# Warm-up in single-pass products, no filler products, the sine table loaded later, and small products in full shape

## The chip, the cores and the metric

The kernel runs on one core of a Trainium2 chip. Its time is the device time of one execution in microseconds (us). The core has a matrix engine (TensorE, PE in the rows; its weight loads are listed apart as PEld), three engines for elementwise work (VectorE or DVE, ScalarE or ACT, GpSimd or POOL) and SP, which mostly starts transfers (DMA). TensorE runs at one of two granted clocks, 1.2 or 2.4 GHz. Three runs of the kernel before took 457.12 us in the median, from 455.9 to 459.17.

## The reference

Three stages follow each other on inputs of batch 2, sequence 768 and width 512 (8 heads of 64), all in fp32.

```
# 1 attention with decay, block by block of the sequence
intra = (q k^T * lam**(i-j) for j <= i) v;  inter = (q * lam**(i+1)) state
state = lam**block * state + (k * lam**(block-1-i))^T v
# 2 transform and feed-forward
u  = x + real(fft over sequence and width of x)
un = (u - mean(u)) / sqrt(var(u) + 1e-6)
x  = u + relu(un @ w_ch1) @ w_ch2            # 512 -> 2048 -> 512
# 3 gated value
gate = sigmoid(conv over 5 steps of x);  out = (gate * (x @ w_val)) @ w_out
```

## The kernel before, in words

The work goes through in three overlapping parts. **Attention** takes each batch in six chunks of 128 positions. A chunk is loaded by four transfers (`load_chunk`, L), and then has score products (`att_S`, S), a multiplication by the decay mask on DVE (`att_pm`, s; tile `pa`), products with v (`att_AV`, A), products with the state (`att_inter`, E) and an update of the state (`att_ST`, T). Chunks are loaded into a ring of three, so a load waits until an earlier chunk has been read. **The transform** of a batch is made of products with cosine and sine tables: `cd` over the width (`fft_D`, XD), `cos` and `sin` over the sequence (`fft_P`, `fft_Q`, XP, XQ), and two small parts, `fft_a384` (XA; what one middle position gives) and `fft_P256` (XK; one middle frequency). **Feed-forward** goes over four blocks of 384 positions (k = 0 to 3) and 16 slices of the 2048 hidden units: `ffn1` (F), relu with the rest to fp32 on DVE (f, h), `ffn2` (G). Before each block stands the norm: mean (Nm), centring (Nc), squares, `ln_var` (Nv, the variance by products with a column of ones) and the square root on DVE and ACT (Nw). Weights are loaded raw and converted on ACT and DVE (names with D). The second batch's attention and transform lie among the first batch's feed-forward.

Products are of two kinds. In fp32r a product is one record in the trace. In fp32 it is two records, and slower. The large products of blocks 1 to 3 are three fp32r products each (`mm3`); those of the transform, the attention and `ffn1` of block 0 are fp32.

The order of all instructions is written out by hand in ORDER, one token for each step: the letters name the method, the numbers its arguments. Each engine takes its instructions in this order, and waits for its operands. A buffer's next writer also waits for its last reader.

Four places matter here. In `setup` eight fp32 products of the identity with `ones` run while the first chunk is loaded, and their result is not read (the warm-up); `pe_fill` (token Z4) makes four more after the first scores. The sine table (`Xcs1`) is the first token of the order, so its transfer stands behind chunk 0. `fft_a384` and `ln_var` take products whose moving operand is a single column. `fft_fx`, `fft_fxh` and `fft_fxl` (Xx, Xh, Xl) make a row of sums and split it into two fp32r parts, which `fft_D` adds to its even half (w = 0) with two products of one row.

Of the kernel before, what the change touches and what calls it, by code (L numbers as in the profile page):

```python
# [34 lines left out]
WARM = 8  # L35
# [8 lines left out]
    "L": "load_chunk", "Z": "pe_fill", "K": "lam_powers", "S": "att_S", "s": "att_pm", "k": "att_kd_act", "A": "att_AV", "E": "att_inter", "T": "att_ST", "t": "att_st", "X": "x_shift",  # L44
    "Xcd": "fft_cd", "Xcs": "fft_cs", "XD": "fft_D", "XA": "fft_a384", "XQ": "fft_Q", "XP": "fft_P", "Xc": "fft_pc",
# [8 lines left out]
    "Kq": "att_qs", "Y": "att_decay", "Xm": "fft_pm", "Xe": "fft_edge", "Xo": "fft_fold", "Xx": "fft_fx", "Xl": "fft_fxl", "Xp": "fft_mp", "Xu": "u_add",  # L54
# [5 lines left out]
Xcs1 S0,0,0 S0,0,1 Z4 L0,1 s0,0,0 s0,0,1 K A0,0 k0,0,0 k0,0,1 L0,2 T0,0 Kq0,1+ e0,0+ k0,1,0 S0,1,0 S0,1,1 t0,0 k0,1,1 T0,1 Y0,1 s0,1,0 L0,3 s0,1,1 A0,1 a0,0 Kq0,2+ t0,1 k0,2,0 S0,2,0  # L60
# [51 lines left out]
class Kern:  # L112
# [16 lines left out]
    def setup(self):  # L129
# [43 lines left out]
        for x in range(2):  # L173
            nc.scalar.copy(self.oddr[:, x * C:(x + 1) * C], self.odd)
# [748 lines left out]
```

## Time and profile before

| | |
|---|---|
| median of three runs | 457.12 us |
| the profiled execution | 459.33 us |
| its span, first to last instruction | 457.5 us |
| mean granted clock of TensorE | 0.989 |
| PE busy | 447.6 us (98%) |
| DVE, ACT, POOL busy | 312.7, 244.6, 129.1 us |
| moved by DMA | 40.45 MB |

Durations come from the profiled execution. In a timeline row the first number is the start, the second the time from the first start to the last end of the merged instructions, and the bracket at the end, where there is one, the idle time before them and what ended it. The ends of products are modelled: a product is shown until its result has left the array, while the next has begun. What a stretch of products costs is therefore read from start to start.

### The profile page before, as it was taken

The numbers are of one execution on the slowest core, as the hardware profiler recorded it, in microseconds if no ns is written. First come the engines' busy times: TensorE is split into PE (matmuls) and PEld (weight loads), VectorE is DVE, ScalarE is ACT, GpSimd is POOL, SyncE is SP. The second block draws the span as 40 slices with busy tenths as digits, with TensorE's granted clock in tenths as the row PEclk, the third lists the DMA queues.
The fourth block names the chain that finished last, engine by engine and source line by source line (L and its number), as shares of the span: only waits on it lengthen the run. The fifth ranks groups of instructions, "written<-read, shape, count | busy, mean of one in ns | idle before, by whom it ended". The sixth has DMA issues, their size and how long they took to land.

```text
span 457.5 us, 7094 instructions
## 1 busy us (share of the span) xinstructions
PE 447.6 (98%) x2752; PEld 396.8 (87%) x2752; DVE 312.7 (68%) x498; ACT 244.6 (53%) x501; POOL 129.1 (28%) x115
## 2 busy tenths in 40 slices
PE   8999999999999999899999999999999999999996
PEld 7887757777658779899999999999999999999994
DVE  5768489887989998885866478813736794222594
ACT  4555566756757765486436357524733844242442
POOL 1132304201041112325263446322523512430230
PEclk9999899889999999999999999999999999999999
DMA  7899951547735340000000000000000010000101
GB/s 266 287 302 318 397 160 65 177 172 255 239 140 185 100 178 1 0 3 0 1 0 24 0 1 23 1 1 24 1 1 0 24 46 1 0 1 24 47 1 69
DMA packets 15861, 40.45 MB, mean 88 GB/s; under 512 B 2012, under 2 KB 4052, under 8 KB 14804
## 3 DMA queue, kind: packets, MB, share of 16 engines
q1 hardware_dynamic: 15540, 39.62, 25.0%
q8 instruction: 21, 0.34, 0.3%
q10 hardware_dynamic: 288, 0.39, 0.3%
q14 instruction: 12, 0.10, 0.1%
HBM read 35.29 MB, written 3.15 MB: 84 GB/s over the span
## 4 chain that ended last, share of the span: by engine, by line
PE 90%; DVE 4%; DMA 2%; SPq 1%; issue 1%; ACT 1%; DVEq 0%; ACTq 0%
PE acc L636 10%; PE acc L638 10%; PE acc L637 10%; PE ph L644 8%; PE ph L638 7%; PE ph L636 7%; PE ph L637 7%; PE pso L636 4%; PE pso L637 4%; PE pso L638 4%; PE pso L373 3%; PE psS L251 3%; PE pso L266 2%; PE pso L277 2%; PE pso L399 2%; PE pso L389 2%
## 5 line engine op out<-in xcount | busy, mean ns | idle before, releaser
L636 PE MATMUL acc<-g,w2s 128*128 128x384 f32 x240 | 83.5, 348 | 1.3 <-DVE tmp L680 1.3
L637 PE MATMUL acc<-g,w2s 128*128 128x384 f32 x240 | 80.5, 335 | 0.0
L638 PE MATMUL acc<-g,w2s 128*128 128x384 f32 x240 | 80.5, 335 | 0.0
L632 POOL TENSOR_TENSOR w2s<-w,w2s 128x512 fp32r<-128x512 f32 x27 | 36.9, 1366 | 145.2 <-ACT w2s L628 130.7
L628 ACT CAST w2s<-w 128x512 fp32r<-128x512 f32 x62 | 37.9, 618 | 42.7 <-PE acc L638 42.7
L665 DVE SCALAR_TENSOR_TENSOR g<-ph,g 128x384 fp32r<-128x384 f32 x60 | 32.8, 553 | 35.3 <-ACT g L660 34.8
L731 DVE SCALAR_TENSOR_TENSOR gate<-u,cw,gate 128x384 f32<-128x384 f32 (+4 forms) x64 | 48.4, 770 | 1.6 <-ACT gate L726 0.9
L636 PEld LDWEIGHTS acc<-g,w2s 128*128 128x128 f32 x240 | 45.1, 188 | 3.7 <-DVE tmp L680 1.6
L614 ACT CAST w1s<-w 128x512 fp32r<-128x512 f32 x48 | 29.6, 618 | 34.5 <-PE ph L638 34.3
L637 PEld LDWEIGHTS acc<-g,w2s 128*128 128x128 f32 x240 | 45.1, 188 | 1.3
L660 ACT ACTIVATE g<-ph 128x384 fp32r<-128x384 f32 x60 | 28.9, 488 | 30.6 <-PE acc L638 17.2
L638 PEld LDWEIGHTS acc<-g,w2s 128*128 128x128 f32 x240 | 45.1, 188 | 0.1
L644 PE MATMUL ph<-uc,w 128*128 128x384 f32 x128 | 45.1, 501 | 0.0
L636 PE MATMUL ph<-hlA,w1s 128*128 128x384 f32 x128 | 43.4, 339 | 0.6 <-DVE g L665 0.6
L638 PE MATMUL ph<-hlA,w1s 128*128 128x384 f32 x128 | 43.1, 337 | 0.2 <-DVE w1s L618 0.2
L637 PE MATMUL ph<-hlA,w1s 128*128 128x384 f32 x128 | 42.9, 335 | 0.0
L618 POOL TENSOR_TENSOR w1s<-w,w1s 128x512 fp32r<-128x512 f32 x21 | 28.2, 1347 | 50.7 <-ACT w1s L614 36.1
L632 DVE TENSOR_TENSOR w2s<-w,w2s 128x512 fp32r<-128x512 f32 x35 | 27.3, 779 | 21.9 <-ACT w2s L628 21.7
L644 PEld LDWEIGHTS ph<-uc,w 128*128 128x128 f32 x128 | 24.8, 197 | 15.0 <-issue 1.4
L618 DVE TENSOR_TENSOR w1s<-w,w1s 128x512 fp32r<-128x512 f32 x27 | 23.0, 859 | 18.6 <-ACT w1s L614 18.6
L636 PEld LDWEIGHTS ph<-hlA,w1s 128*128 128x128 f32 x128 | 24.0, 188 | 1.3 <-DVE g L665 0.9
L638 PEld LDWEIGHTS ph<-hlA,w1s 128*128 128x128 f32 x128 | 24.0, 188 | 0.8 <-DVE w1s L618 0.8
(212 smaller groups left out, 957.4 us busy)
## 6 DMA issues: line engine op xcount, KB each, us to landing
raw<-in_w_dram SPq DMA_DIRECT2D x16, 1024.0 KB, 5.0
ldqk<-in_qT_dram SPq DMA_DIRECT2D x12, 256.0 KB, 5.7
ldqk<-in_k_dram SPq DMA_DIRECT2D x12, 256.0 KB, 5.8
ldv<-in_v_dram SPq DMA_DIRECT2D x12, 256.0 KB, 5.8
ldkT<-in_kT_dram SPq DMA_DIRECT2D x11, 256.0 KB, 6.3
out_dram<-o SPq DMA_DIRECT2D x11, 256.0 KB, 2.0
raw<-in_wv_dram SPq DMA_DIRECT2D x2, 1024.0 KB, 5.0
raw<-in_wo_dram SPq DMA_DIRECT2D x2, 1024.0 KB, 4.7
```

Source lines behind the costliest of these rows:

```text
L251: nc.tensor.matmul(r["pss"][t][:, a, :], r["kT"][hp, a, :], r["qT"][hp, a, :], start=True, stop=True)
L614: self.nc.scalar.copy(w[:, 0], self.raw1(f))
L618: eng.tensor_tensor(w[:, 1], self.raw1(f), w[:, 0].bitcast(F32), op=ALU.subtract)
L628: self.nc.scalar.copy(w[:, 0], self.raw2(f))
L632: eng.tensor_tensor(w[:, 1], self.raw2(f), w[:, 0].bitcast(F32), op=ALU.subtract)
L636: nc.tensor.matmul(out, lh, rh, start=start, stop=False)
L637: nc.tensor.matmul(out, lh, rl, start=False, stop=False)
L638: nc.tensor.matmul(out, ll, rh, start=False, stop=stop)
L644: self.nc.tensor.matmul(ph, self.raw1(f)[:, t], self.uc[k][:, t], start=(t == 0), stop=(t == 3))
L660: self.nc.scalar.activation(g[:, 0], self.ph[(k, f)], AF.Relu)
L665: self.nc.vector.scalar_tensor_tensor(g[:, 1], self.ph[(k, f)], 0.0, g[:, 0].bitcast(F32), op0=ALU.max, op1=ALU.subtract)
L731: self.nc.vector.scalar_tensor_tensor(gp[:, o:TB], x, w, gp[:, o:TB], op0=ALU.mult, op1=ALU.add)
```

## The change

Five things change. The warm-up becomes ten fp32r products of 512 equal columns of `ones`; for this `ones` is cast to `onesr` on DVE at the start, where ACT did it before. `pe_fill` and its token Z4 are gone. `Xcs1` stands behind the load of the fourth chunk. In `fft_a384` and `ln_var` each product has 128 columns where it had one: the same column 128 times over, or all of `ones`; `fft_P256` takes 128 columns of weights where it took one. And `fft_fx` writes its row into partition 0 of the folded tile `F` (a row that the odd half multiplies by zeros), so that `fft_D` adds one fp32 product with 128 equal columns, written to every second column; the two fp32r products of one row, `fft_fxh` and `fft_fxl` are gone.

```
-WARM = 8
+WARM = 10
...
+        self.onesr = p.tile([P, P], F32R, name="onesr", tag="onesr")
+        nc.vector.tensor_copy(self.onesr, self.ones)
...
         for n in range(WARM):
-            nc.tensor.matmul(warm[:, 0:P], ident, self.ones, start=True, stop=True)
+            nc.tensor.matmul(warm, self.onesr, self.onesr[:, 0:1].to_broadcast([P, 512]), start=True, stop=True)
...
-    def pe_fill(self, n):
-        ps = self.ps_o.tile([P, 512], F32, name="pso2", tag="pso2")
-        for _ in range(n):
-            self.nc.tensor.matmul(ps[:, 0:P], self.ident, self.ones, start=True, stop=True)
...
     def fft_fx(self, eng, b):
         z = self.PM[b]
-        self.fx[b] = self.tmp()[0:1]
-        eng.tensor_tensor(self.fx[b], z[0:1, 1, 0, 0:HS], z[:, :, :, S:HS:-1][0:1, 1, 0, :], op=ALU.add)
...
+        eng.tensor_tensor(self.F[b][0:1, 1, 0, :], z[0:1, 1, 0, 0:HS], z[:, :, :, S:HS:-1][0:1, 1, 0, :], op=ALU.add)
...
     def fft_a384(self, b):
...
-        for g, (c0, cw) in enumerate(((0, 128), (128, 128), (256, 1))):
-            for a in range(2):
-                nc.tensor.matmul(ps[:cw, g:g + 1], cd[:, a, c0:c0 + cw], z[:, 0, a, HS:HS + 1], start=(a == 0), stop=(a == 1 and g > 1))
+        for g in range(3):
+            x = [(cd[:, a, g * P:(g + 1) * P], z[:, 0, a, HS:HS + 1]) for a in range(2)]
             if g < 2:
-                nc.tensor.matmul(ps[:, g:g + 1], self.odd[0:1, 0:128], z[0:1, 1, 0, HS:HS + 1], start=False, stop=True)
+                x.append((self.odd, z[:, 1, 0, HS:HS + 1]))
+            for n, (w, y) in enumerate(x):
+                nc.tensor.matmul(ps[:, g * P:(g + 1) * P], w, y.to_broadcast([P, P]), start=(n == 0), stop=(n == len(x) - 1))
...
     def fft_D(self, b, j, w):
...
         if w == 0:
-            for x in range(2):
-                nc.tensor.matmul(ps[:, 0:256], self.fxr[b][x][:, sl], self.oddr, start=False, stop=(x == 1))
+            nc.tensor.matmul(ps[:, 1:256:2], F[:, 1, 0, sl], self.odd[:, 1:2].to_broadcast([P, C]), start=False, stop=True, skip_group_check=True)
...
     def fft_P256(self, b):
...
-            self.nc.tensor.matmul(ps[0:1, 0:HS + 1], self.AB[b][:, j, 256:257], self.cs[0][:, j, :], start=(j == 0), stop=(j == 2))
+            self.nc.tensor.matmul(ps[:, 0:HS + 1], self.AB[b][:, j, 256:384], self.cs[0][:, j, :], start=(j == 0), stop=(j == 2))
...
     def ln_var(self, k):
...
-                self.nc.tensor.matmul(ps[:, t:t + 1], x[:, t * P:(t + 1) * P], self.ones[:, 0:1], start=(d == 0), stop=(d == len(qs) - 1))
+                self.nc.tensor.matmul(ps[:, t * P:(t + 1) * P], x[:, t * P:(t + 1) * P], self.ones, start=(d == 0), stop=(d == len(qs) - 1))
...
-Xcs1 S0,0,0 S0,0,1 Z4 L0,1 s0,0,0 s0,0,1 K A0,0 k0,0,0 k0,0,1 L0,2 T0,0 Kq0,1+ e0,0+ k0,1,0 S0,1,0 S0,1,1 t0,0 k0,1,1 T0,1 Y0,1 s0,1,0 L0,3 s0,1,1 A0,1 a0,0 Kq0,2+ t0,1 k0,2,0 S0,2,0
+S0,0,0 S0,0,1 L0,1 s0,0,0 s0,0,1 Kl A0,0 k0,0,0 k0,0,1 L0,2 T0,0 Kq0,1+ e0,0+ k0,1,0 S0,1,0 S0,1,1 t0,0 k0,1,1 T0,1 Y0,1 s0,1,0 L0,3 Xcs1 s0,1,1 A0,1 a0,0 Kq0,2+ t0,1 k0,2,0 S0,2,0
```

TensorE at the start of the program, before. Rows name the line, the result, its operands and the result's shape; L251 is S, L266 is A, L310 is T.

```order
L153 MATMUL pso_95<-ones,ident 128x128 x8
L251 MATMUL psS<-ldqk,ldkT_81 128x128 x8
L198 MATMUL pso_141<-ones,ident 128x128 x4
L266 MATMUL pso<-pa,ldv 64x128 x8
L310 MATMUL psd<-ldv,kd 64x64 x8
L251 MATMUL psS<-ldqk,ldkT_81 128x128 x8
```

The same place now (the lines have moved: L243 is S, L258 is A, L302 is T).

```order
L155 MATMUL pso_97<-onesr 128x512 x10
L243 MATMUL psS<-ldqk,ldkT_81 128x128 x8
L258 MATMUL pso<-pa,ldv 64x128 x8
L302 MATMUL psd<-ldv,kd 64x64 x8
L243 MATMUL psS<-ldqk,ldkT_81 128x128 x8
```

Between the first scores and the first products with v nothing is left for TensorE to do.

TensorE at the first batch's transform, before: `fft_a384` (L357, L359), T and S of two chunks, and `fft_D` (L373, L376).

```order
L357 MATMUL pso_648<-pm,cd 128x1 x2
L359 MATMUL pso_648<-pm,odd 128x1
L357 MATMUL pso_648<-pm,cd 128x1 x2
L359 MATMUL pso_648<-pm,odd 128x1
L357 MATMUL pso_648<-pm,cd 1x1 x2
L310 MATMUL psd<-ldv,kd 64x64 x8
L251 MATMUL psS<-ldqk,ldkT_81 128x128 x8
L373 MATMUL pso_700<-cd,F 128x257 x2
L376 MATMUL pso_700<-oddr,tmp 128x256 x2
L373 MATMUL pso_715<-cd,F 128x257 x2
L376 MATMUL pso_715<-oddr,tmp 128x256 x2
```

The same place now.

```order
L344 MATMUL pso_642<-pm,cd 128x128 x2
L344 MATMUL pso_642<-pm,odd 128x128
L344 MATMUL pso_642<-pm,cd 128x128 x2
L344 MATMUL pso_642<-pm,odd 128x128
L344 MATMUL pso_642<-pm,cd 128x128 x2
L302 MATMUL psd<-ldv,kd 64x64 x8
L243 MATMUL psS<-ldqk,ldkT_81 128x128 x8
L358 MATMUL pso_689<-cd,F 128x257 x2
L360 MATMUL pso_689<-odd,F 128x128
L358 MATMUL pso_703<-cd,F 128x257 x2
L360 MATMUL pso_703<-odd,F 128x128
```

The eight products of `fft_a384` keep their places with 128 columns each, and one product stands where the two of one row stood.

DVE at the second batch's fold, before (L342 is `fft_fx`, L349 `fft_fxl`, L337 the fold, L665 the rest of relu).

```order
L326 TENSOR_TENSOR pm<-u_128 128x2x384
L342 TENSOR_TENSOR tmp<-pm 1x384
L665 SCALAR_TENSOR_TENSOR g<-ph,g 128x384 x2
L632 TENSOR_TENSOR w2s<-w_0_780,w2s 128x512
L502 SCALAR_TENSOR_TENSOR w_1_930<-raw,w_1_930 128x1024
L349 TENSOR_TENSOR tmp<-tmp 1x384
L326 TENSOR_TENSOR pm<-u_128 128x2x384
L337 TENSOR_TENSOR F<-pm 128x384 x3
```

The same place now (L333 is `fft_fx`, L329 the fold).

```order
L318 TENSOR_TENSOR pm<-u_127 128x2x384
L649 SCALAR_TENSOR_TENSOR g<-ph,g 128x384 x2
L616 TENSOR_TENSOR w2s<-w_0_766,w2s 128x512
L486 SCALAR_TENSOR_TENSOR w_1_916<-raw,w_1_916 128x1024
L318 TENSOR_TENSOR pm<-u_127 128x2x384
L329 TENSOR_TENSOR F<-pm 128x384 x3
L333 TENSOR_TENSOR F<-pm 1x384
```

`fft_fx` has moved behind the fold, and `fft_fxl` is gone.

## Rows read from the trace of the kernel before

**Rows 1.** The page: TensorE's busy time (part 1), and the chain that ended last.

```profile
PE 447.6 (98%) x2752; PEld 396.8 (87%) x2752; DVE 312.7 (68%) x498; ACT 244.6 (53%) x501; POOL 129.1 (28%) x115
...
PE 90%; DVE 4%; DMA 2%; SPq 1%; issue 1%; ACT 1%; DVEq 0%; ACTq 0%
```

**Rows 2.** Timeline of PE, 0 to 14 us.

```profile
1.51 3.78 PE L153 MATMUL pso<-ones,ident 128*128 128x128 f32 x16 [1.51 <-POOL ident masks.py:199]
6.02 2.08 PE L251 MATMUL psS<-ldqk,ldkT 64*128 64x128 f32 x16 [0.73 <-DMA ldqk<-in_qT_dram]
8.03 2.07 PE L198 MATMUL pso<-ones,ident 128*128 128x128 f32 x8
10.03 1.51 PE L266 MATMUL pso<-pa,ldv 128*64 128x128 f32 x16
...
11.94 1.16 PE L251 MATMUL psS<-ldqk,ldkT 64*128 64x128 f32 x16
13.03 0.69 PE L310 MATMUL psd<-ldv,kd 128*64 128x64 f32 x16
```

**Rows 3.** Timeline of DVE, 4 to 15 us.

```profile
4.99 2.63 DVE L158 TENSOR_TENSOR_SCAN mask<-lam_b,ident 128x128 f32<-128x128 f32 x8 [4.99 <-DMA lam_b<-in_lam_dram]
...
8.10 1.29 DVE L257 TENSOR_TENSOR pa<-psS,mask 128x512 f32<-128x512 f32 x2 [0.47 <-PE psS L251]
...
11.59 0.42 DVE L286 COPY xs<-pso 128x256 f32<-128x256 f32 x1 [0.20 <-PE pso L266]
...
13.13 1.29 DVE L257 TENSOR_TENSOR pa<-psS,mask 128x512 f32<-128x512 f32 x2 [0.62 <-PE psS L251]
```

**Rows 4.** Chain of waits, 90 to 92 us: one fp32r product of 384 columns.

```profile
91.10 0.17 PE acc L638
```

**Rows 5.** The page, DMA issues: KB and us to landing.

```profile
sin<-in_sin_dram SPq DMA_DIRECT2D x1, 577.5 KB, 6.2
```

**Rows 6.** One-us windows: length, busy us of each engine, granted clock, DMA share, GB/s.

```profile
46.00:47.00 1.00, 1.00 (x12) 0.88 (x10) 0.00 (x0) 1.00 (x6) 0.94 (x2) 0.50 1.00 379
...
101.00:102.00 1.00, 1.00 (x4) 0.81 (x3) 0.51 (x1) 0.44 (x2) 0.00 (x0) 0.50 0.00 0
```

**Rows 7.** Timeline of PE, 42 to 51 us: the first transform.

```profile
42.66 0.58 PE L357 MATMUL pso<-pm,cd 128*128 128x1 f32 x4 [0.89 <-DMA cd<-in_cd_dram]
...
44.48 0.69 PE L310 MATMUL psd<-ldv,kd 128*64 128x64 f32 x16
45.10 2.08 PE L251 MATMUL psS<-ldqk,ldkT 64*128 64x128 f32 x16
47.11 1.79 PE L373 MATMUL pso<-cd,F 128*128 128x257 f32 x4
48.83 0.50 PE L376 MATMUL pso<-oddr,tmp 1*128 1x256 f32 x2
49.26 1.13 PE L373 MATMUL pso<-cd,F 128*128 128x257 f32 x4
```

**Rows 8.** Timeline of PE, 64 to 69 us: `fft_Q` and `fft_P256`.

```profile
64.81 2.21 PE L389 MATMUL pso<-sin,AB 128*128 128x385 f32 x6
66.95 2.10 PE L424 MATMUL pso<-cos,AB 128*1 128x385 f32 x6
```

**Rows 9.** Timeline of PE, 80 to 110 us: variance, `ffn1`, the second transform.

```profile
80.19 2.91 PE L567 MATMUL pso<-ones,tmp 128*128 128x1 f32 x24
82.97 6.91 PE L644 MATMUL ph<-uc,w 128*128 128x384 f32 x16
...
99.54 3.68 PE L373 MATMUL pso<-cd,F 128*128 128x256 f32 x8
...
104.55 5.33 PE L644 MATMUL ph<-uc,w 128*128 128x384 f32 x16
```

**Rows 10.** Chain of waits, 172 to 174 us: the variance of block 1.

```profile
172.67 0.56 PE pso L567 x6
```

**Rows 11.** Timeline of DVE, 104 us.

```profile
104.00 0.69 DVE L489 TENSOR_SCALAR w<-w 128x1024 f32<-128x1024 f32 x1 [2.48 <-ACT w L485]
```

More of the change, by code (lines that the diff above doesn't have):

```diff
@@ L53 @@
 GPS = {
-    "Kq": "att_qs", "Y": "att_decay", "Xm": "fft_pm", "Xe": "fft_edge", "Xo": "fft_fold", "Xx": "fft_fx", "Xl": "fft_fxl", "Xp": "fft_mp", "Xu": "u_add",
+    "Kq": "att_qs", "Y": "att_decay", "Xm": "fft_pm", "Xe": "fft_edge", "Xo": "fft_fold", "Xx": "fft_fx", "Xp": "fft_mp", "Xu": "u_add",
     "Ns": "ln_sum", "Nl": "ln_lo", "Na": "ln_acc", "u": "split1l", "v": "split2l", "R": "resid", "Ml": "m_lo", "Mk": "m_gvl",
@@ L166, in setup @@
         self.lam_hc, self.zero = lam_hc, zero
-        self.onesr = p.tile([P, P], F32R, name="onesr", tag="onesr")
-        nc.scalar.copy(self.onesr, self.ones)
-        self.odd = self.fft.tile([1, C], F32, name="odd", tag="odd")
+        self.odd = self.fft.tile([P, C], F32, name="odd", tag="odd")
         nc.gpsimd.memset(self.odd, 0.0)
-        nc.gpsimd.memset(self.odd[:, 1:C:2], 1.0)
-        self.oddr = self.fft.tile([1, 2 * C], F32R, name="oddr", tag="oddr")
-        for x in range(2):
-            nc.scalar.copy(self.oddr[:, x * C:(x + 1) * C], self.odd)
+        nc.gpsimd.memset(self.odd[0:1, 1:C:2], 1.0)
         self.U = [p.tile([P, 4, S], F32, name=f"u{b}", tag=f"u{b}") for b in range(B)]
@@ L340, in fft_fx @@
         z = self.PM[b]
-        self.fx[b] = self.tmp()[0:1]
-        eng.tensor_tensor(self.fx[b], z[0:1, 1, 0, 0:HS], z[:, :, :, S:HS:-1][0:1, 1, 0, :], op=ALU.add)
-    def fft_fxh(self, b):
-        self.fxr[b] = [self.tmp(dt=F32R)[0:1] for _ in range(2)]
-        self.nc.scalar.copy(self.fxr[b][0], self.fx[b])
-    def fft_fxl(self, eng, b):
-        eng.tensor_tensor(self.fxr[b][1], self.fx[b], self.fxr[b][0].bitcast(F32), op=ALU.subtract)
+        eng.tensor_tensor(self.F[b][0:1, 1, 0, :], z[0:1, 1, 0, 0:HS], z[:, :, :, S:HS:-1][0:1, 1, 0, :], op=ALU.add)
     def fft_a384(self, b):
@@ L372, in fft_D @@
         for a in range(2):
-            nc.tensor.matmul(ps[:, 0:n], F[:, w, a, sl], cd[:, a, o:o + n], start=(a == 0), stop=(a == 1 and w == 1))
+            nc.tensor.matmul(ps[:, 0:n], F[:, w, a, sl], cd[:, a, o:o + n], start=(a == 0), stop=(a == 1), skip_group_check=True)
         if w == 0:
-            for x in range(2):
-                nc.tensor.matmul(ps[:, 0:256], self.fxr[b][x][:, sl], self.oddr, start=False, stop=(x == 1))
+            nc.tensor.matmul(ps[:, 1:256:2], F[:, 1, 0, sl], self.odd[:, 1:2].to_broadcast([P, C]), start=False, stop=True, skip_group_check=True)
     def fft_Dev(self, eng, b, j, w):
         if b not in self.AB:
-            self.AB[b] = self.fft.tile([P, 3, 514], F32, name="AB", tag="AB")
+            self.AB[b] = self.fft.tile([P, 3, 513], F32, name="AB", tag="AB")
         n = 257 if w == 0 else 256
-        o = 0 if w == 0 else 258
+        o = 0 if w == 0 else 257
         eng(self.AB[b][:, j, o:o + n], self.psD[(b, j, w)][:, 0:n])
@@ L386, in fft_Q @@
         ps = self.psQ[(b, g)] = self.ps_o.tile([P, 512], F32, name="pso2", tag="pso2")
-        o = 258 + 128 * g
+        o = 257 + 128 * g
         for j in range(3):
```

98 lines of the change are left out of this document (49 added, 49 removed), and 2 rows, old and new, of the table PLAIN.

## The prediction

> **What bounds the kernel now.** I read the page first. TensorE is busy for 98% of the span and holds 90% of the chain that ended last; DVE has 4% of the chain and DMA 2% [rows 1]. A gain must therefore come out of TensorE's own stream: fewer products, less idle time, or the same products at the higher clock. Then I read the timeline of PE at the places that the diff touches, and the windows of one microsecond for the granted clock there.
>
> The clock is at its lower level in four stretches. The first is the start. The record of the clock begins only at its first change, so here durations tell: the first score products take 2.08 us, the same sixteen records at 11.94 take 1.16, and the filler is still at the slow pace until 10.03 [rows 2]. The other three stand in the windows at 0.50: about 45.1 to 48.5, 82.6 to 86.0 and 99.7 to 103.1 us, of which a window of the first and of the third is shown [rows 6]. Ahead of each fall TensorE had been working through products of one column: eight of `fft_a384` from 42.66 to 44.48, after 0.89 us of waiting for `cd` [rows 7]; twelve of `ln_var` from 80.19, with no idle time [rows 9]; and eight of `fft_a384` again ahead of the third, with none either. The three products of `ln_var` in block 1, 0.56 us [rows 10], and the two microseconds of `fft_P256`, whose moving operand has 385 columns and whose weights have one [rows 8], were followed by no fall.
>
> **The start.** Before, TensorE ends the filler at 10.03 and takes up A, although `pa` was ready at 9.39 (8.10 and 1.29) [rows 2, 3]. Without the filler A starts at 9.39 at the latest. If the scores ran at the higher clock, they would end near 7.1, and `pa` would be held by the mask scans, which end at 7.62 (4.99 and 2.63): A at 8.95 [rows 3]. Behind A the next stop is DVE, which must make `pa` of chunk 1; in that stretch it waited 0.20 us for A and 0.62 us for S of chunk 1 [rows 3]. So A of chunk 1 can come forward by 0.82 us if the first scores stay slow, and by some 0.45 more if they are fast: 1.25. From there TensorE has hardly any idle time up to 41.8 us, and the shift stays. The wait for `cd` at 42.66 moves along, since its transfer is issued behind copies of attention's results. I take **−1.0 us**. The worst end is a loss: nothing fills the time from the end of the scores to A, so the clock may rise later than it does now. If A, T and S of chunk 1 (10.03 to 13.03, 3.0 us [rows 2], in part slow already) ran at half the clock, this would cost some 2 us and the term would be **+1.0**.
>
> The warm-up itself lies beside the load of chunk 0, which ends TensorE's wait at 6.02 [rows 2]. A one-pass product of 384 columns takes 0.17 us at the higher clock [rows 4], so one of 512 takes 0.23, ten take 2.3, and at half the clock 4.6. `onesr` needs `ones` and a cast instead of the identity, so the start stays near 1.5 or a little earlier, and the end lies between 3.8 and 6.1 us. Nothing is queued behind it but the scores: 0 us, 0.1 at worst. DVE's cast runs long before the scans' operand arrives at 4.99.
>
> The sine table is 577.5 KB [rows 5]. In SP's queue its transfer now stands behind chunks 1 to 3, which come 1.5 us earlier at the 379 GB/s of a full window [rows 6] (an estimate), and ahead of chunk 5, whose load starts only when S of chunk 2 has read its buffer. It is first used by `fft_Q` at 57.5 us. What hides it is 40 us of attention: 0 us. Without the earlier chunks the 0.82 us above might not all come.
>
> **The three falls.** If 128 columns keep the clock up where one column lets it fall, each stretch runs at the pace of its like at the higher clock. First fall: S 2.08 against 1.16, and D 1.79 against 1.13 [rows 2, 7], −0.92 and −0.66, **−1.58**. Second: sixteen records of `ffn1` take 6.91 us, and 5.33 twenty microseconds later [rows 9]: **−1.58**. Third: eight records of D in 3.68; two groups of four at the higher clock take 2 × 1.06 and 0.07 for the last one's drain (1.13 is a group with its drain) [rows 7, 9]: **−1.49**. Behind the first, DVE and ACT only evict and convert, and DMA has delivered `cos` and the chunks some microseconds ahead. Behind the second, DVE is nearly full until it waits 2.48 us for ACT, up to 104.00 [rows 11], and ACT had waited for TensorE. TensorE waited for DVE nowhere between 80 and 110 us, so I let the gain stay, though this margin is the thinnest.
>
> **The price of the new shapes.** The trace has no fp32 product of 128 × 128 with full rows at the higher clock. From below: 384 columns take 5.17/8 = 0.646 us [rows 9], a third of it is 0.215. From above: S makes two such products side by side in 1.09/4 = 0.27 us [rows 2]. I take 0.24, between the two, since neither row is nearer. Then:
> `fft_D`: the two one-row products took 48.83 to 49.26, 0.43 us [rows 7]; one product instead, six times: 6 × (0.24 − 0.43) = **−1.14** (−1.3 to −1.0).
> `fft_a384`: 42.66 to 44.48 is 1.82 us [rows 7], taken alike in the second batch; eight at 0.24 are 1.92: **+0.2** for both (−0.2 to +0.7).
> `ln_var` of block 0: 80.19 to 82.97 is 2.78; twelve at 0.24 are 2.88: **+0.1** (−0.2 to +0.5). Blocks 1 to 3: 0.56 [rows 10] against 0.72, three times: **+0.5** (+0.3 to +0.8).
> `fft_P256`: 2.10 with one column of weights, 2.21 with 128 in `fft_Q` [rows 8]: **+0.2** for both batches.
> The folds: `fft_fx` on DVE moves behind the fold that D waits for, 0.55 us, and two single-row operations ahead of it go. In the first batch S of 2 us lies between the fold and D, in the second about 1 us; hidden, and 0.5 us if that cover were gone. The removed casts and subtractions on ACT and POOL were off the path.
>
> A rule that speaks against this part: the Trainium skill (TensorE: Matmul & The Clock Gate, Back-to-back issue gap) gives about 60 cycles for up to 64 columns and 134 for 128, a ratio of 2.2; by it the 37 products at some 0.23 us would cost some 10 us more (an estimate from that ratio), and the sum would end near 463. The rows don't show such cheap small products: one column takes 0.56/6 = 0.093 us per record [rows 10], and 128 columns by the lower bound 0.107.
>
> **The sum.** −1.0 − 1.58 − 1.58 − 1.49 − 1.14 + 0.2 + 0.1 + 0.5 + 0.2 = −5.8. Against the profiled execution: 459.33 − 5.8 = 453.5. That execution is as slow as the slowest of the three runs (459.17), and the fastest is 3.3 us below, about what two falls cost. An execution with fewer falls has less to gain, and the end without any should be the same; I take **453.3**, 0.8% under the median of 457.12.
>
> **The rivals.** (a) The falls stay. TensorE was never idle ahead of the second and third [rows 9]; if it is not the single columns that bring them, equal columns change nothing. Then only the start, D and the extra columns are left: 459.33 − 1.0 − 1.14 + 1.0 = 458.2 by the profile, 457 by the median. The Trainium skill (TensorE: Matmul & The Clock Gate, Why this matters for your kernels) tells only of idle gaps as what lets the clock fall; by that rule single columns are innocent, and this rival would follow. Against it stands that long streams of wide products nowhere fell. (b) The first fall alone stays, since the wait for `cd` of 0.89 us [rows 7] remains ahead of it, or grows as TensorE arrives earlier at a nearly full DMA: 455.0. (c) The clock rises later at the start: +1.0 for −1.0, 455.3. (d) Slower: wide columns are paid on top of the weight load instead of beside it. The place is the 37 products with 128 columns and the 6 in D; the price is 0.215 each on top of some 0.23. The 37 cost 8 us more, D gains nothing: 459.33 − 5.65 + 8.0 = 461.7. This is where the rule on columns above would lead. It decides from 0.24 + 5.8/43 = 0.37 us a product on. That weight loads show a busy time beside the products' (87% and 98%) [rows 1] speaks against it; that `ffn1` has no visible load time in 0.646 us does too.
>
> **How the numbers follow.** The forecast has 0.58, with a range of its own from 451.3 (new products at 0.215, the start at −1.25, and both clocks' ends) to 454.5; (a) 0.12, (b) 0.11, (c) 0.10, (d) 0.05, and 0.04 for a larger gain. About 1% is what a measurement of this kernel can tell from no change; that is 452.5 and 461.7. Roughly half of the forecast's range and most of the larger gain lie under 452.5: faster 0.36. Slower by over 1% holds half of (d) and what I have not thought of: 0.05. Within 1%: 0.59. The range from 450.3 to 457.2 leaves out (d) and parts of (a).
>
> **What would show it.** In the changed kernel's windows the clock should be 1.00 at 45 to 48, at 80 to 86 and at 96 to 103 us. A of chunk 0 should start between 8.9 and 9.5 us, with 1.05 us for its sixteen records instead of 1.51, and S of chunk 1 some 1 us earlier than 11.94. The eight products of `fft_a384` should take 1.7 to 2.2 us, the twelve of `ln_var` 2.6 to 3.2, one product beside D 0.2 to 0.27. The prediction is wrong if a window at 0.50 remains there, if S of chunk 1 still takes 2 us, if PE shows new waits for DVE between 80 and 120 us, or if the new products take over 0.35 us.

## The result, and the profile after

| | before | after |
|---|---|---|
| median (six runs each) | 457.85 us | 451.91 us |
| lowest to highest | 455.9 to 459.17 | 451.17 to 452.48 |
| the profiled execution, its span | 459.33, 457.5 us | 451.17, 449.4 us |
| its mean granted clock | 0.989 | 1.000 |

The ratio is 0.9887, with a 95% interval of 0.9851 to 0.9922: faster by 1.1%, or 5.9 us in the median, where 453.3 us had been predicted, 3.8 us or 0.8% under the 457.12 us of the first three runs. The measured 451.91 us lies inside the range (450.3 to 457.2). Between the two profiled executions the span is 8.1 us shorter. Medians here and below are of all runs; the ratios leave out runs more than 1.5% above the fastest of the same kernel.

The page of the changed kernel, the lines that answer to [rows 1], and TensorE's granted clock in 40 slices:

```profile
PE 438.9 (98%) x2738; PEld 391.8 (87%) x2738; DVE 313.5 (70%) x498; ACT 243.6 (54%) x496; POOL 128.3 (29%) x114
...
PEclk9999999999999999999999999999999999999999
```

TensorE is as full as before, with 8.7 us less work to be busy with, and no slice shows a lower clock; the record of the clock begins only at its first rise, here at 6.2 us. One-microsecond windows of the changed kernel where [rows 6] had 0.50 (length, busy time of PE, PEld, DVE, ACT and POOL, granted clock, DMA share, GB/s):

```profile
45.00:46.00 1.00, 1.00 (x6) 0.89 (x7) 0.95 (x2) 0.71 (x3) 0.00 (x0) 1.00 0.86 315
79.00:80.00 1.00, 1.00 (x4) 0.60 (x4) 1.00 (x1) 1.00 (x1) 0.18 (x1) 1.00 0.91 369
94.00:95.00 1.00, 1.00 (x7) 0.87 (x6) 0.97 (x2) 0.51 (x3) 0.00 (x0) 1.00 0.00 0
```

In this execution the three falls are gone. The timeline of PE at the start, changed kernel (L155 warm-up, L243 S, L258 A), against [rows 2]:

```profile
1.26 4.63 PE L155 MATMUL pso<-onesr 128*128 128x512 f32 x10 [1.26 <-DVE onesr L149]
6.00 1.25 PE L243 MATMUL psS<-ldqk,ldkT 64*128 64x128 f32 x16
8.26 0.43 PE L258 MATMUL pso<-pa,ldv 128*64 128x128 f32 x2 [1.02 <-DVE pa L249]
8.86 0.98 PE L258 MATMUL pso<-pa,ldv 128*64 128x128 f32 x13 [0.16 <-DVE pa L249]
...
10.34 1.16 PE L243 MATMUL psS<-ldqk,ldkT 64*128 64x128 f32 x16
```

The first scores take 1.25 us instead of 2.08: the clock has risen by about 6.2 us, at the end of a warm-up without a gap. TensorE then stands for 1.02 us until DVE has made the first half of `pa`, and keeps the clock here. S of chunk 1 starts at 10.34 instead of 11.94, 1.60 us earlier. DVE's timeline there, to set beside [rows 3]:

```profile
7.54 1.26 DVE L249 TENSOR_TENSOR pa<-psS,mask 128x512 f32<-128x512 f32 x2
...
11.53 1.29 DVE L249 TENSOR_TENSOR pa<-psS,mask 128x512 f32<-128x512 f32 x2
```

All three waits of DVE in [rows 3] (0.47, 0.20 and 0.62 us) are gone; the copy that had the middle one now starts at 10.72 without a wait. The timeline of PE in the transforms and the norm of the changed kernel (L344 `fft_a384`, L358 and L360 `fft_D`, L383 `fft_P`, L551 `ln_var`, L628 `ffn1`), against [rows 7, 9]:

```profile
41.17 0.68 PE L344 MATMUL pso<-pm,cd 128*128 128x128 f32 x4 [0.96 <-DMA cd<-in_cd_dram]
...
43.74 1.16 PE L243 MATMUL psS<-ldqk,ldkT 64*128 64x128 f32 x16
44.83 1.13 PE L358 MATMUL pso<-cd,F 128*128 128x257 f32 x4
45.80 0.38 PE L360 MATMUL pso<-odd,F 128*128 128x128 f32 x2
46.02 1.03 PE L358 MATMUL pso<-cd,F 128*128 128x257 f32 x4
46.89 0.38 PE L360 MATMUL pso<-odd,F 128*128 128x128 f32 x2
...
51.60 2.11 PE L383 MATMUL pso<-cos,AB 128*128 128x385 f32 x6
...
76.16 2.84 PE L551 MATMUL pso<-ones,tmp 128*128 128x128 f32 x24
78.84 5.33 PE L628 MATMUL ph<-uc,w 128*128 128x384 f32 x16
...
90.77 0.60 PE L344 MATMUL pso<-pm,cd 128*128 128x128 f32 x4
...
92.55 1.03 PE L358 MATMUL pso<-cd,F 128*128 128x257 f32 x4
...
96.46 5.32 PE L628 MATMUL ph<-uc,w 128*128 128x384 f32 x16
```

`ffn1` has 5.33 us where it had 6.91, and S before D 1.16 where it had 2.08. A new product costs 0.22 us (45.80 to 46.02; twelve in 78.84 − 76.16 = 2.68; eight in 92.55 − 90.77 = 1.78). Of the kernel before, the second batch's `fft_a384` and D (L357, L373, L376), the rows that [rows 9] leaves out:

```profile
96.30 0.50 PE L357 MATMUL pso<-pm,cd 128*128 128x1 f32 x4
...
98.05 1.14 PE L373 MATMUL pso<-cd,F 128*128 128x257 f32 x4
...
103.16 0.49 PE L376 MATMUL pso<-oddr,tmp 1*128 1x256 f32 x2
```

The 8.1 us, read from the start of one step to the start of the same step in the other trace:

| stretch | predicted | measured |
|---|---|---|
| start, to the first `fft_a384` | −1.0 | −1.49 |
| first batch: `fft_a384`, T, S, D, to `fft_P` | −2.05 | −2.46 |
| `fft_P`, `fft_Q`, `fft_P256` and on to `ln_var` | +0.1 | −0.08 |
| `ln_var` of block 0 | +0.1 | −0.10 |
| the `ffn1` behind it | −1.58 | −1.59 |
| up to the second `fft_a384` | 0 | +0.19 |
| second batch: `fft_a384` and D | −1.96 | −2.56 |
| from there to the end (`ln_var` of blocks 1 to 3) | +0.6 | 0.0 |
| sum | −5.8 | −8.1 |

### The profile page after: what moved, and what is told of

It is laid out like the page before. It is cut to its first block, busy times and chain, and to the rows that moved or that the text cites. A ratio compares the mean times of both kernels' runs of the same rounds, so it can differ in the third digit from the quotient of the medians.

```text
span 449.4 us, 7061 instructions
## 1 busy us (share of the span) xinstructions
PE 438.9 (98%) x2738; PEld 391.8 (87%) x2738; DVE 313.5 (70%) x498; ACT 243.6 (54%) x496; POOL 128.3 (29%) x114
## 4 chain that ended last, share of the span: by engine, by line
PE 89%; DVE 5%; DMA 3%; issue 1%; SPq 1%; ACT 0%; DVEq 0%; ACTq 0%
PE acc L622 10%; PE acc L620 10%; PE acc L621 10%; PE ph L628 8%; PE ph L622 8%; PE ph L620 7%; PE ph L621 7%; PE pso L620 4%; PE pso L621 4%; PE pso L622 4%; PE pso L358 2%; PE psS L243 2%; PE pso L258 2%; PE pso L383 2%; PE pso L373 2%; PE pso L269 2%
## 5 line engine op out<-in xcount | busy, mean ns | idle before, releaser
L616 DVE TENSOR_TENSOR w2s<-w,w2s 128x512 fp32r<-128x512 f32 x35 | 28.7, 820 | 21.8 <-ACT w2s L612 21.7
L628 PE MATMUL ph<-uc,w 128*128 128x384 f32 x128 | 43.7, 488 | 0.0
L628 PEld LDWEIGHTS ph<-uc,w 128*128 128x128 f32 x128 | 23.8, 190 | 14.8 <-DVE g L649 0.7
L478 ACT ACTIVATE raw<-raw 128x1024 int32<-128x1024 uint32 (+1 forms) x21 | 23.4, 1118 | 3.4 <-DMA raw<-in_w_dram 2.8
L620 PEld LDWEIGHTS ph<-hlA,w1s 128*128 128x128 f32 x128 | 24.0, 188 | 1.3 <-DVE g L649 0.9
```

The lines of the kernel that those rows point to most:

```text
L478: self.nc.scalar.activation(w, w.bitcast(U32), AF.Copy, bias=-0.5 + 2.0 ** -17, scale=2.0 ** -29 - 2.0 ** -47)
L616: eng.tensor_tensor(w[:, 1], self.raw2(f), w[:, 0].bitcast(F32), op=ALU.subtract)
L620: nc.tensor.matmul(out, lh, rh, start=start, stop=False)
L628: self.nc.tensor.matmul(ph, self.raw1(f)[:, t], self.uc[k][:, t], start=(t == 0), stop=(t == 3))
```

## The experiments

The theory: single columns let the clock fall, full shapes keep it up, and the start and D bring something each. Its rivals: the new start makes the gain, or the falls come from idle time and not from shapes. Three sets of kernels ran, each set on one chip with runs of the kernel before beside it.

| kernel | median us | ratio to before, 95% | mean granted clock of its runs |
|---|---|---|---|
| set 1: before (33 runs) | 456.41 | | 0.981 to 0.999 |
| e1_start_only | 458.96 | 1.0012 [0.9969, 1.0056] | 0.978 to 0.996 |
| e2_shapes_only | 451.73 | 0.9900 [0.9868, 0.9932] | 0.999 to 1.0 |
| e3_var_one_column | 452.86 | 0.9928 [0.9895, 0.9961] | 0.992 to 1.0 |
| e4_a384_one_column | 453.15 | 0.9935 [0.9906, 0.9965] | 0.991 to 0.998 |
| set 2: before (23 runs) | 457.58 | | 0.981 to 0.999 |
| after_again | 451.99 | 0.9898 [0.9847, 0.9948] | 0.996 to 1.0 |
| e8_old_D | 454.41 | 0.9951 [0.9924, 0.9979] | 0.994 to 1.0 |
| e9_new_D_only | 455.93 | 0.9981 [0.9946, 1.0017] | 0.989 to 1.0 |
| e7_sine_first | 452.01 | 0.9898 [0.9850, 0.9947] | 0.994 to 1.0 |
| set 3: before (11 runs) | 457.89 | | 0.984 to 0.996 |
| e5_old_warmup_no_fill | 452.65 | 0.9878 [0.9846, 0.9911] | 0.995 to 0.999 |
| e6_fp32_warmup_same_length | 452.50 | 0.9890 [0.9857, 0.9923] | 0.994 to 0.996 |
| e11_one_pass_filler | 451.95 | 0.9863 [0.9839, 0.9887] | 0.999 to 1.0 |
| e12_filler_cd_earlier | 452.01 | 0.9876 [0.9846, 0.9907] | 0.996 to 1.0 |

The clock column tells how much a run lost to falls, but not where: that only a profile shows, and each kernel has one. One stretch of 3.4 us at half the clock is 1.7 us of lost work, 0.0037 of the span; a lower clock in the last 1.6 to 1.9 us of an execution (e7, e6, e8) takes up to 0.002 more. Thirty of the 33 runs of before in set 1 lie on such steps: 453.4 to 454.7 us at a mean clock of 0.999 (no fall behind the start), 454.6 to 456.1 at 0.996 (one), 456.0 to 456.8 at 0.992 (two), 457.6 to 460.1 at 0.989 (three), up to 461.4 at 0.981. Three lie between the steps (0.993 to 0.995). The number of falls differs from run to run of the same program; that is the spread of the kernel before.

**e1_start_only** has the kernel before with the new start alone.

```
-WARM = 8
+WARM = 10
-            nc.tensor.matmul(warm[:, 0:P], ident, self.ones, start=True, stop=True)
+            nc.tensor.matmul(warm, self.onesr, self.onesr[:, 0:1].to_broadcast([P, 512]), start=True, stop=True)
-Xcs1 S0,0,0 S0,0,1 Z4 L0,1
+S0,0,0 S0,0,1 L0,1
...
+L0,3 Xcs1
```

> The kernel before with the new start alone: ten one-pass products, no filler, the sine table behind the fourth chunk; the small products keep one column. If single columns let the clock fall, the falls stay and only the start's gain comes: about 1.5 us under the kernel before, 456.3. If the falls went because the start moved everything, they are gone here too: about 452.

It gains nothing: its ratio is 1.0012, its median lies 2.5 us above that of before, and no run has a mean clock over 0.996. So the falls remain. Its windows and the PE timeline of its first transform:

```profile
50.00:51.00 1.00, 1.00 (x14) 0.78 (x15) 0.52 (x2) 0.15 (x1) 0.00 (x0) 0.50 1.05 383
...
58.00:59.00 1.00, 1.00 (x5) 0.78 (x5) 0.97 (x2) 0.45 (x2) 0.00 (x0) 1.00 0.01 2
```

```profile
41.09 0.58 PE L357 MATMUL pso<-pm,cd 128*128 128x1 f32 x4 [0.70 <-DMA cd<-in_cd_dram]
...
44.90 2.08 PE L373 MATMUL pso<-cd,F 128*128 128x257 f32 x4
```

Behind the single columns the clock falls at 44.3 and stays down to 57.9 us, 13.7 us instead of the 3.4 of before, with PE busy throughout. Its profile has no later fall.

**e2_shapes_only** has the new shapes and D, with the old start: eight fp32 warm-up products, the filler, the sine table first.

```
-WARM = 10
+WARM = 8
-            nc.tensor.matmul(warm, self.onesr, self.onesr[:, 0:1].to_broadcast([P, 512]), start=True, stop=True)
+            nc.tensor.matmul(warm[:, 0:P], ident, self.ones, start=True, stop=True)
-S0,0,0 S0,0,1 L0,1
+Xcs1 S0,0,0 S0,0,1 Z4 L0,1
```

> The changed kernel with the start of before: eight fp32 products of the identity, the filler, the sine table first. If single columns let the clock fall, there is no fall behind the small products, the clock rises first near 10 us, and the time is about 1.5 us over the changed kernel: 453.4. If the start did it, the falls are back: about 456 to 457.

The whole gain is here: 451.73 us, and not one of its ten runs shows a fall. A row of PE's timeline:

```profile
42.80 0.68 PE L349 MATMUL pso<-pm,cd 128*128 128x128 f32 x4 [1.13 <-DMA cd<-in_cd_dram]
```

In this profile it reaches `fft_a384` 1.63 us later than the changed kernel's, as the old start should; yet its median is no worse than the 451.91 and 451.99 us of the changed kernel in other sets. The 1.5 us that its expectation gave to the start don't show.

**e3_var_one_column** and **e4_a384_one_column** give back single columns in the changed kernel: e3 in `ln_var` (first pair of lines), e4 in `fft_a384` (second pair).

```
-  nc.tensor.matmul(ps[:, t * P:(t + 1) * P], x[...], self.ones, ...)
+  nc.tensor.matmul(ps[:, t * P:t * P + 1], x[...], self.ones[:, 0:1], ...)
-  nc.tensor.matmul(ps[:, g * P:(g + 1) * P], w, y.to_broadcast([P, P]), ...)
+  nc.tensor.matmul(ps[:, g * P:g * P + 1], w, y, ...)
```

> The changed kernel, with one column in the products of the variance again. If single columns let the clock fall, one stretch of half clock returns behind the variance of block 0 and nowhere else: about 1.6 us slower, 453.5, less some 0.1 for each later block if one column is cheaper there. If not: 451.9 or a little less.

> The changed kernel, with one column in the eight products of the middle position again. If single columns let the clock fall, two stretches of half clock return, behind these products in each batch: about 3 us slower, 455. If the wait for the table cd brings the first fall, it alone returns or none: 451.9 to 453.5.

e4 is 1.4 us behind e2, and 11 of its 12 runs have a mean clock of 0.996 or less; of the changed kernel's 12 runs (in two other sets) three have. A row of PE's timeline, and a window each of the first and the second batch:

```profile
41.60 0.58 PE L344 MATMUL pso<-pm,cd 128*128 128x1 f32 x4 [1.34 <-DMA cd<-in_cd_dram]
```

```profile
45.00:46.00 1.00, 1.00 (x12) 0.94 (x10) 0.00 (x0) 1.00 (x5) 0.00 (x0) 0.50 1.05 395
...
93.00:94.00 1.00, 1.00 (x12) 1.00 (x11) 0.98 (x3) 0.11 (x1) 0.00 (x0) 1.00 1.00 414
```

The clock falls in the first batch, from 43.9 to 47.3 us, behind a wait of 1.34 us and the single columns; in the second, with the same columns and no wait, it does not. Its expectation gave 455 us to two falls that single columns bring back, and up to 453.5 to one that the wait for `cd` brings: the 453.15 us and the one fall are the second case. What its other runs lost their clock to, no profile shows. e3 falls nowhere in its profile, where a fall behind the variance had been expected, and seven of its 12 runs are at 0.996 or below. Whether those falls stand behind `ln_var` or at the start (below) its runs don't tell, so the share of `ln_var` stays open.

**after_again** is the changed kernel once more.

> The changed kernel as it is, on the chip of the next three. About 452, no stretch of half clock after the start.

451.99 us, as the first time. Three of its six runs lie at 0.996 (453.1 to 454.1 us), three at 0.998 to 1.0 (450.6 to 450.9). So the changed kernel has a fall left in some runs, against the expectation; its profile, of one of the others, doesn't show where.

**e8_old_D** puts the two one-row products back into D, with their row's split; **e9_new_D_only** gives the kernel before the new D and nothing else.

```
-  nc.tensor.matmul(ps[:, 1:256:2], F[:, 1, 0, sl], self.odd[:, 1:2].to_broadcast([P, C]), start=False, stop=True, ...)
+  for x in range(2):
+      nc.tensor.matmul(ps[:, 0:256], self.fxr[b][x][:, sl], self.oddr, start=False, stop=(x == 1))
...
-Xo0,0,0+ Xo0,1,1 Dl0 T1,2 Xo0,0,1+ S1,3,0 a1,2 S1,3,1 Xo0,1,0+ Xx0+
+Xo0,0,0+ Xx0+ Xo0,1,1 Dl0 T1,2 Xo0,0,1+ Xh0 S1,3,0 a1,2 Xl0 S1,3,1 Xo0,1,0+
```

> The changed kernel with the old D: two products of one row each instead of one full product (and the split of the row into two parts). If the products of one row only lengthen a fall that single columns begin, there is no fall here, and the time is 1.2 us over the changed kernel, the price of the products: about 453. If they can begin a fall themselves, the windows at D show 0.50, and the time is 454 to 458.

> The kernel before with the new D alone; start, single columns and filler as before. If the products of one row keep the clock down once it has fallen, falls still begin behind the single columns, but each lasts about 3.4 us and none 13: about 454 to 455, with less spread between runs than before. If single columns alone count, only the 1.2 us of the products come: about 456.

e8 takes 454.41 us, 2.4 more than after_again, where 1.2 had been expected. e9 takes 455.93, 1.65 less than before in the median, but its interval (0.9946 to 1.0017) takes in no change; of its two expectations it is the second, about 456. PE's timeline of e8 (the rows at 55.41 and 101.63 are the first records of what follows D):

```profile
43.97 0.68 PE L307 MATMUL pso<-pm,cd 128*128 128x128 f32 x4 [1.92 <-DVE F L284]
...
47.62 1.13 PE L321 MATMUL pso<-cd,F 128*128 128x257 f32 x4
48.69 0.50 PE L324 MATMUL pso<-oddr,tmp 1*128 1x256 f32 x2
49.12 1.13 PE L321 MATMUL pso<-cd,F 128*128 128x257 f32 x4
50.18 0.50 PE L324 MATMUL pso<-oddr,tmp 1*128 1x256 f32 x2
...
55.41 0.81 PE L347 MATMUL pso<-cos,AB 128*128 128x385 f32 x2
...
96.93 1.03 PE L321 MATMUL pso<-cd,F 128*128 128x257 f32 x4
...
98.31 2.00 PE L321 MATMUL pso<-cd,F 128*128 128x256 f32 x8
100.24 0.49 PE L324 MATMUL pso<-oddr,tmp 1*128 1x256 f32 x2
...
101.63 1.78 PE L592 MATMUL ph<-uc,w 128*128 128x384 f32 x5
```

The two one-row products take 0.43 us (48.69 to 49.12) against 0.22 for the new one, near what the sum had. But the four records ahead of them take 49.12 to 50.18, 1.06 us, and in the changed kernel 0.87 (46.02 to 46.89). From the first product of D to what follows D (47.62 to 55.41 and 96.93 to 101.63), e8 has 7.79 and 4.70 us in the two batches, the changed kernel (44.83 to 51.60 and 92.55 to 96.46) 6.77 and 3.91: 1.8 us for the new D, not 1.14. No fall follows the one-row products at the higher clock here, and ten of e8's twelve runs have a mean clock of 0.998 or more, so they don't start one by themselves. The fall that this profile does have, at 8.9 us, is that of e7 below. The wait of 1.92 us is put down to DVE's fold, which ends at 43.88; but `cd`, issued at 36.27 and 7.6 us under way, lands at that time too, and `fft_a384` reads `cd` and not the fold.

e9's PE timeline shows one more thing:

```profile
42.15 0.61 PE L305 MATMUL pso<-pm,cd 128*128 128x1 f32 x4
```

Here single columns come without any wait ahead, and this execution (453.0 us, clock 1.0) has no fall anywhere. The mean clocks of the other 11 of its 12 runs (0.989 to 0.996) are those of one to three falls, so the new D doesn't take them away. With e1, e2 and e8 this separates the parts: falls are common where the shapes of `fft_a384`, `ln_var` and `fft_P256` are old (before, e1, e9), and rare where they are new, be the start old (e2) or D old (e8).

**e7_sine_first** moves the sine table back to the first place of the order.

```
-S0,0,0 S0,0,1 L0,1 ... L0,3 Xcs1 s0,1,1
+Xcs1 S0,0,0 S0,0,1 L0,1 ... L0,3 s0,1,1
```

> The changed kernel with the sine table loaded behind chunk 0 again. If the later load lets attention start earlier, scores of chunk 1 start later by up to 1.5 us, or keys are waited for, and the time is 0.5 to 1 us over the changed kernel. If the table's load was hidden anyway, no difference within 0.3 us.

452.01 against 451.99 us: the place of the sine table is worth nothing that shows. Its profiled execution caught what is probably the fall that the changed kernel has in some runs, in PE's timeline and a window of the start:

```profile
8.23 0.43 PE L258 MATMUL pso<-pa,ldv 128*64 128x128 f32 x2 [1.20 <-DVE pa L249]
8.83 1.75 PE L258 MATMUL pso<-pa,ldv 128*64 128x128 f32 x13 [0.17 <-DVE pa L249]
...
11.58 1.47 PE L243 MATMUL psS<-ldqk,ldkT 64*128 64x128 f32 x16
```

```profile
9.00:10.00 1.00, 1.00 (x12) 1.00 (x14) 1.00 (x4) 0.00 (x0) 0.00 (x0) 0.50 1.05 385
```

The clock rises at 5.4 us, TensorE stands 1.20 us for `pa`, and from 8.9 to 12.3 it runs at half the clock: A takes 1.75 us instead of 0.98, and S of chunk 1 starts 1.24 us later than at 10.34.

Why here and not in the changed kernel's own profile is not shown. In nine profiles with the same ten warm-up products the clock rose anywhere between 4.1 and 7.4 us (e3 4.1; e7 5.4; e8 5.5; after_again 6.0; after 6.2; e4 6.4; e11 6.5; e1 6.7; e12 7.4). Of these, the fall at 8.9 us is in the two where it had risen at 5.4 and 5.5. The wait for `pa` doesn't tell them apart: it was 1.20 and 1.10 us in e7 and e8, and 1.09 and 1.11 in e3 and after_again, which kept the clock.

**e5_old_warmup_no_fill** and **e6_fp32_warmup_same_length** change the warm-up of the changed kernel: e5 has the eight old products without the filler (first added line, WARM = 8), e6 three fp32 products of 448 columns, as long as the ten (second, WARM = 3).

```
-            nc.tensor.matmul(warm, self.onesr, self.onesr[:, 0:1].to_broadcast([P, 512]), start=True, stop=True)
+            nc.tensor.matmul(warm[:, 0:P], ident, self.ones, start=True, stop=True)
+            nc.tensor.matmul(warm[:, 0:448], self.ones, self.ones[:, 0:1].to_broadcast([P, 448]), start=True, stop=True)
```

> The changed kernel with the eight fp32 products of before as its warm-up, and no filler. If the kind of the warm-up's products decides when the clock first rises, it rises later than the 6.2 us of the changed kernel, at 10 us or, without the filler, past 12: scores of chunk 1 near 12 us, 1 to 3 us over the changed kernel, 453 to 455. If the kind doesn't matter, within 0.5 us of it.

> The changed kernel with a warm-up of three fp32 products of 448 equal columns, which at the lower clock last as long as the ten one-pass products (4.5 us). If it is the single pass that raises the clock early, the clock rises near 10 us here and the time is 1 to 3 us over the changed kernel. If length alone does, the rise comes near 6 us and the time is that of the changed kernel, 452.

PE's timeline of e5, and below it the first scores of e6 and of e3, whose warm-up is that of the changed kernel:

```profile
12.26 2.08 PE L243 MATMUL psS<-ldqk,ldkT 64*128 64x128 f32 x16
...
44.80 0.98 PE L344 MATMUL pso<-pm,cd 128*128 128x128 f32 x4 [1.88 <-DMA cd<-in_cd_dram]
```

```profile
5.85 1.16 PE L243 MATMUL psS<-ldqk,ldkT 64*128 64x128 f32 x16 [0.15 <-DMA ldqk<-in_qT_dram]
...
5.99 1.16 PE L243 MATMUL psS<-ldqk,ldkT 64*128 64x128 f32 x16 [0.90 <-DMA ldqk<-in_qT_dram]
```

With the short warm-up and no filler the clock rises only at 14.3 us, and S of chunk 1 takes 2.08 us: this is rival (c), though the median, 452.65, is hardly worse. With three long fp32 products it rises at 5.4, before the scores, inside the 4.1 to 7.4 us of the ten fp32r products. So the single pass isn't needed for an early rise. Nor does a gap ahead of the scores prevent it: in e3 the clock had risen at 4.1, and the scores run at full pace behind a gap of 0.90 us, longer than the 0.73 of before [rows 2]. What keeps the clock down longer behind the eight old products no run separates. All four runs of e6 lie at 0.994 to 0.996, and its profile has the same fall as e7's, 8.8 to 12.3, behind a wait of 1.23 us.

e5 shows a second thing. Its profiled execution waited 1.88 us for `cd`, and the clock fell from 45.0 to 48.4 us with 128 columns in every product.

**e11_one_pass_filler** and **e12_filler_cd_earlier** act on what was found. Both have the changed kernel with a filler of four fp32r products of 512 columns behind the first scores (not read); e12 also issues `cd` some places earlier (the last pair of lines).

```
+    def pe_fill(self, n):
+        ps = self.ps_o.tile([P, 512], F32, name="pso2", tag="pso2")
+        for _ in range(n):
+            self.nc.tensor.matmul(ps, self.onesr, self.onesr[:, 0:1].to_broadcast([P, 512]), start=True, stop=True)
-S0,0,0 S0,0,1 L0,1
+S0,0,0 S0,0,1 Z4 L0,1
-Xe0,0 X0,1 ... A1,1 Xcd Xe0,1
+Xe0,0 Xcd X0,1 ... A1,1 Xe0,1
```

> The changed kernel with four one-pass products of 512 equal columns, not read, between the first scores and A, where TensorE is idle for a microsecond. If that idle time is what makes the clock fall again near 9 us in half of the runs, no run shows it here, and the median is about 0.8 us under the changed kernel, 451, with a smaller spread. If the fall near 9 us has another cause, no difference.

> As the one before, with the transfer of the table cd issued ahead of the copies of the first batch's second half. If TensorE's wait of 1 us for cd at 41 us is on the path, it goes and the time is up to 1 us under the kernel with the filler, 450. If the copies, now behind cd, hold the fold instead, no gain.

PE's timeline of e11, and below it that of e12:

```profile
7.43 1.14 PE L195 MATMUL pso<-onesr 128*128 128x512 f32 x4
8.50 1.56 PE L263 MATMUL pso<-pa,ldv 128*64 128x128 f32 x15
...
10.56 1.16 PE L248 MATMUL psS<-ldqk,ldkT 64*128 64x128 f32 x16
```

```profile
43.16 0.71 PE L301 MATMUL pso<-pm,cd 128*128 128x128 f32 x4 [1.98 <-DVE pm L275]
```

In e11 all six runs are at 0.999 or more, for 0.2 us of a later S (10.56 against 10.34). With the six of e12, whose one fall is at 44.9, that is twelve runs with the filler and no fall at 9 us; of 18 without it (after, after_again, e7) five have a mean clock of 0.996 or less. This speaks for the filler, but the runs were on different chips, and where the five fell only e7's profile shows. e11's ratio, 0.9863, is the lowest of all; 451.95 us is no better than the changed kernel by anything that can be measured here. In e12 `cd` no longer ends the wait, but `pm` does, 1.98 us, since copies stand behind the earlier `cd`; and in this execution the clock falls at 44.9. Nothing is gained in the median.

## Why the prediction was right

**The falls.** This was the main term, −4.65 of −5.8 us, and it held against an execution with three falls: −1.58 and −1.58 by the rows, −1.7 (−0.92 in S and −0.75 in D) and −1.6 in the trace for the first two. For the third I had put −1.49 by two groups at 1.06; in e8, which has the old D at the higher clock, the same records take 98.31 to 100.24, 1.93 us, where before had 99.54 to 103.16, 3.62, so it was −1.7. Rival (a) is refuted by e2, in which shapes and D alone took every fall away in ten runs, and by e8, where the old D brings none back at the transforms, while the new D alone (e9) and the new start alone (e1) leave falls. What the Trainium skill (TensorE: Matmul & The Clock Gate, Why this matters for your kernels) tells of idle gaps, weighed there for this rival, is half of it. The clock does fall behind idle time with full shapes too (e5 and e12 behind 1.88 and 1.98 us, e7 behind 1.20), though not each time. But the second and third fall of before had none ahead [rows 9], and e2 kept `cd`'s wait and lost the falls. Which of the single columns brings the second and the third is not shown: no profile with one part restored (e3, e4) or one part changed (e1, e9) has a fall there.

**The wait for cd**, rival (b), is real but rarer than I feared. With 128 columns, profiled executions kept the clock behind waits of 0.96, 1.13, 1.92 and 2.04 us (after, e2, e8, e3) and lost it behind 1.88 and 1.98 (e5, e12, which waited for `pm`). What decides between these is open; the length of the wait doesn't. With single columns it fell behind 0.70, 0.89 and 1.34 us (e1, before, e4) and not without a wait (e9). That in the first batch both count, the wait and the columns, fits these rows, but each case is one execution.

**The start** was mis-sized, and its gain is less sure than its term. By the profile it is −1.49 and not −1.0. I had let A begin at 8.95 behind the whole of `pa`; it begins with the first half, at 8.26, ahead of the 8.9 to 9.5 that I had named as a sign, and DVE's three waits, 1.29 us together, all vanish. In the median nothing of it shows. e1 with the new start alone is level with before by its ratio, and e2 with the old start is level with the changed kernel. Two things can take it back. In some runs the clock falls at 9 us, which is rival (c) in another form: the clock doesn't rise later but falls again, behind the wait for `pa` that nothing fills (in the profiles of e6, e7 and e8; in none of the runs with a filler). And TensorE reaches `fft_a384` at 40.2 to 40.4 us in after, after_again, e3 and e11, but starts it at 41.17, 40.83, 42.30 and 40.75, whenever `cd` has landed. e3's row in PE's timeline:

```profile
42.30 0.68 PE L344 MATMUL pso<-pm,cd 128*128 128x128 f32 x4 [2.04 <-DMA cd<-in_cd_dram]
```

My sentence that this wait "moves along" with the start holds in some executions and not in others. That this is what the medians lose is argued from these rows and not shown; e12 took the wait away and got another in its place.

**D** is the other term with a wrong size: −1.14 predicted, −1.8 by e8. The step that failed counted only the replaced products (0.43 each time, −1.26 at the measured 0.22) and left the 257-column records beside them at 1.06 us a group. They take 0.87 to 0.97 beside the new product (46.02 to 46.89, 44.83 to 45.80).

**The price of the shapes** was 0.22 us, near the lower bound (0.215). Eight single-column products of the second batch took 1.75 us in the kernel before (96.30 to 98.05), eight with 128 columns take 1.78; in the first batch it was 1.82 [rows 7] and 1.95 (41.17 to 43.12). So `fft_a384` cost +0.13 and +0.03 instead of +0.1 each, `ln_var` of block 0 −0.1 instead of +0.1, and the last 353 us nothing instead of +0.6. The ratio of 2.2 between 128 columns and a few in the Trainium skill (TensorE: Matmul & The Clock Gate, Back-to-back issue gap) is given there for products without their weight loads, and isn't met by these fp32 products, each with weights of its own: here it is 1.0. Rival (d) is refuted; it needed 0.37 us a product.

**DVE's margin** behind the second fall, which I called the thinnest, held: the `ffn1` there has 5.33 us and PE waits for nothing between 76 and 120 us.

**The median.** I put an execution without falls at 453.3 us for the changed kernel. Before has such runs too, 453.4 to 454.7 us in set 1, and the changed kernel lies at 450.6 to 452.5. To compare all runs, take from each time what its mean clock lost, (1 − clock) × span; this is an estimate. Then before comes to 453.1 to 453.5 us in the three sets, e1 to 453.6, e8 to 454.0, e9 to 452.4, e2 to 451.7 and the changed kernel to 451.6 and 451.1. So nothing of the start shows; some 1.5 to 2 us beside the falls are gone, about what D saves in e8's trace (by these figures alone D would be worth 0.8 in e9 and 2.9 in e8); and the rest of the 5.9 us, about 4, is the falls, of which a run of before has two or three. That the sum of the other terms came near what they brought is partly luck: the start was put too high for the medians, D too low, and the extra columns cost less than the 1.0 us I gave them. My line of 1% lay at 452.5 us, and I gave 0.36 to a time under it, as it came out, and 0.59 to one that can't be told from no change.

## What to carry to other kernels

A clock that falls while TensorE is full is a cost that no wait shows: look at the granted clock by windows, see which products stand ahead of each fall, and count falls over several runs before putting a price on them. These fp32 products of one column are no cheaper than those of 128 (0.22 us each), so broadcasting the column cost nothing that shows here, and the falls went with it. It doesn't make up for idle gaps like the two met here (1.2 us behind the first scores, 1.9 us ahead of `fft_a384`), behind which the clock fell in some executions; with a filler in the first no run of twelve fell there, and an earlier operand for the second brought another wait. An edit at the start may be worth only what the next wait for a transfer lets through; here that is argued, not shown.

## What the runs showed of the hardware that was not expected

- One-row fp32r products didn't start a fall (e8), but in e1 a fall that ran through a D with them lasted 13.7 us, with PE 100% busy, against 3.4 us in before. Only one profile shows it that long, and that the one-row products are the reason is not shown.
- The fp32 groups of 257 columns take 1.06 to 1.07 us with one-row fp32r products between them and 0.87 to 0.97 with a full fp32 product. Why is not settled.
- With one and the same warm-up the clock rose at 4.1 to 7.4 us (ten fp32r products, nine profiles). It rose at 5.4 with three wide fp32 products (e6), at 10.3 to 10.9 with the old eight and their filler (e2, e9, before), and at 14.3 with the old eight alone (e5).
- The fall at 8.9 us is in the three profiles with a rise at 5.4 or 5.5 (e6, e7, e8), and in none with an earlier or later one, behind waits for `pa` of much the same length. What sets the time of the rise no run shows.
- The same program loses from run to run nothing or as much as five stretches of 1.7 us (before, mean clock 0.999 to 0.981), which is 8 us of spread.
